# Last value sums behind the first output products, and rows and operands of the next row pairs prepared earlier

## Chip, cores and metric

The kernel runs on one core of one Trainium2 chip. The metric is device time in microseconds (us), from the start to the end of one execution. A core has a matrix engine (TensorE, PE in the profile), a vector engine (VectorE, DVE), an activation engine (ScalarE, ACT), a general engine (GpSimd, POOL) and a queue that starts data transfers (SyncE, SP). Each of them runs its own instructions strictly in the order in which the program issued them, and waits for the others by semaphores.

## What is computed

Two independent blocks over 2048 rows of width 576 are written side by side. Block A is attention with a compressive memory: 32 heads of 18 features, four segments of 512 rows.

```python
for s in range(4):
    logits = qs @ ks.T * scale + mask          # 512 x 512 per head
    a_dot  = softmax(logits) @ vs
    a_mem  = (phi(qs) @ M) / (phi(qs) @ z + 1e-6)
    outs.append(g * a_mem + (1 - g) * a_dot)
    M, z = M + phi(ks).T @ vs, z + phi(ks).sum()
a = concat(outs) @ wo                          # 2048 x 576
```

Block B is the real part of a two-dimensional discrete Fourier transform, written as products with dense matrices:

```python
a, b = x @ hid_re.T, x @ hid_im.T
y = seq_re @ a - seq_im @ b                    # 2048 x 576
out = concat([a_of_block_A, y], axis=-1)
```

## The kernel before

All products of 32-bit numbers are made from two parts each: a high part, rounded to a format that TensorE multiplies at full rate, and a low part, the difference. So the usual three instructions prepare an operand: ScalarE copies the high part, VectorE or GpSimd subtracts it from the original to get the low part.

**Stages.** First come the projections and the memory (`project_qk`, `project_v`, `lookup`). Then one long loop mixes the attention proper with block B: `attention()` is a generator that goes over 64 pairs of heads (a step `p` for each, with eight slots), and after every slot as many pieces of the generator `dense()` (the Fourier products, line 583) are issued as keep the two in step by planned costs. What `dense()` still has left when `attention()` is through is issued by a drain loop, `for t in d: tick()` (line 1215). Last comes `output_stage()`, the product with `wo`.

**The helper `later(n, fn, ...)`** puts an operation off by `n` calls of `tick()`. A `tick()` is called once for every slot and for every piece of the drain loop; `while due: tick()` issues all that is still put off.

**The end of attention.** A group `G` is four heads of one segment. `pv` multiplies probabilities by values into a PSUM tile; `pv_out` (line 1073) makes of it, in five VectorE operations (lines 1083 to 1092), the weighted output of two heads and adds it to the group's tile `og`. After the second pair of a group, `turn_out` (line 1100) transposes `og` in blocks into `ogt` (two VectorE operations), writes it to the DRAM tensor `od[s]`, and copies the last eight columns to `ogl` (GpSimd). After every fourth group `turn_tails` (line 1115) transposes these (`oglt`), writes them to `odt[s]`, and a DMA from DRAM to DRAM brings them, twice, into `od[s]`. So `od[3]` is complete only after the very last of these transfers. The last call of `pv_out` is made in the last step of `attention()`.

**The output stage.** The 16 row tiles are multiplied in pairs: pair `n` is tiles `n` and `n + 8`, so pairs 0 to 3 need the segments 0 and 2 and pairs 4 to 7 need the segments 1 and 3. A pair is multiplied by seven products instead of eight (a Strassen scheme). `o_pair(n)` asks for the rows of a pair, from `od`, into two of the four `craw` buffers, which are used before that for block B's rows; pairs 0 and 1 use other buffers (`oraw`) and are asked for earlier. `left(n)` prepares the pair's left operands in steps (sums of blocks, high and low parts): on VectorE lines 832, 833, 837, 844 and 849, on ScalarE 830, 834, 838, 839, 842 and 845, on GpSimd 829, 836, 841 and 847 (for pair 0 on VectorE). `output_stage` then issues for each `n`, in this order on TensorE, `p1(n)`, `p6(n)`, `p4(n-1)`, `p5(n)`, `p3(n-1)`, `p7(n)`, `p2(n)`: `p1`, `p6` and `p5` are six matmuls each, the others eight. Between them stand the steps of `left(n + 1)` and the operations that take the products out of PSUM: line 877 after `p1` (ScalarE), 883 after `p6`, 889 after `p4`, 900 after `p3`, 907 and 908 after `p7` (VectorE), 914 after `p2` (ScalarE). `p7(n)` writes the same PSUM bank as `p6(n)`, so it has to wait for line 883. Stores go out on SP's queue from line 866.

Of the kernel before, what the change touches and what calls it, by code (L numbers as in the profile page):

```python
# [40 lines left out]
def infini_attention_and_fnet(ctx: ExitStack, tc: tile.TileContext, xT, wqk, w8, wv, wo, beta, xtT, cT, hT, out):  # L41
# [49 lines left out]
    def tick():  # L91
        clock[0] += 1
        for fn, a in due.pop(clock[0], ()):
            fn(*a)
# [595 lines left out]
    def o_pair(n):  # L690
        for t in (n, n + 8):
            o_load(t, lambda: sr.tile([P, 5, P], F32, name="craw", bufs=4))
# [116 lines left out]
    def left(n):  # L809
        one, two = O.pop(n), O.pop(n + 8)  # L810
        add = pool if n else dve
        if n:
            def new():
                return wide.tile([P, 4, P], F32R, name="wide", tag="wide")

            ah, al, s1, s2, l1, l2, a22, tl = (new() for _ in range(8))
            tl = tl[:, :2]
            t = sa.tile([P, 4, 2, P], F32, name="ls", tag="ptt", bufs=2)
        else:
            a, hi, lo = (sa.tile([P, 8, P], F32R, name="l0", tag="pf", bufs=3) for _ in range(3))  # L820
            ah, al, s1, s2, l1, l2 = (x[:, i:i + 4] for x in (a, hi, lo) for i in (0, 4))
            b = sa.tile([P, 6, P], F32R, name="lb", tag="hl", bufs=2)
            a22, tl = b[:, :4], b[:, 4:]
            t = sa.tile([P, 4, 2, P], F32, name="ls", tag="hl", bufs=2)
        LEFT[n] = {"A11": (ah[:, :2], al[:, :2]), "A12": (ah[:, 2:], al[:, 2:]), "A22": (a22[:, :2], a22[:, 2:]),
                   "S1": (s1[:, :2], l1[:, :2]), "S2": (s1[:, 2:], l1[:, 2:]), "S3": (s2[:, :2], l2[:, :2]),
                   "S4": (s2[:, 2:], l2[:, 2:]), 1: tl[:, 0], 2: tl[:, 1]}
        halves = [t[:, i:i + 2].rearrange("p a k x -> p (a k) x") for i in (0, 2)]
        add.tensor_tensor(t[:, 0], two[:, :2], two[:, 2:4], OP.add)
        act.activation(ah, one[:, :4], AF.Copy)  # L830
        yield
        dve.tensor_tensor(t[:, 2], one[:, :2], two[:, :2], OP.subtract)
        dve.tensor_tensor(al, one[:, :4], ah.bitcast(F32), OP.subtract)
        act.activation(a22[:, :2], two[:, 2:4], AF.Copy)
        yield
        add.tensor_tensor(t[:, 1], t[:, 0], one[:, :2], OP.subtract)
        dve.tensor_tensor(a22[:, 2:], two[:, 2:4], a22[:, :2].bitcast(F32), OP.subtract)
        act.activation(tl[:, 0], one[:, 4], AF.Copy)
        act.activation(tl[:, 1], two[:, 4], AF.Copy)
        yield  # L840
        add.tensor_tensor(t[:, 3], one[:, 2:4], t[:, 1], OP.subtract)
        act.activation(s1, halves[0], AF.Copy)
        yield
        dve.tensor_tensor(l1, halves[0], s1.bitcast(F32), OP.subtract)
        act.activation(s2, halves[1], AF.Copy)
        for i, o in enumerate((one, two)):
            add.tensor_tensor(tl[64:, i], o[64:, 4], tl[64:, i].bitcast(F32), OP.subtract)
        yield
        dve.tensor_tensor(l2, halves[1], s2.bitcast(F32), OP.subtract)
        yield  # L850
# [17 lines left out]
    def output_stage():  # L868
        C, Z, U = slice(0, 288), slice(288, 576), {}

        def p1(n):
            u = U[n] = [sb.tile([P, 576], F32, name="u", tag="ab", bufs=10) for _ in range(4)]
            u += [bank("s", [P, L], F32, "s")[:, :288], bank("t", [P, L], F32, "t")[:, :288],
                  ps.tile([P, 288], F32, name="d", bufs=3)]
            seventh(u[4], n, "A11", "B11", True)
            yield
            act.activation(u[0][:, C], u[4], AF.Copy)

        def p6(n):
            u = U[n]  # L880
            seventh(u[5], n, "S2", "T2", True)
            yield
            dve.tensor_tensor(u[0][:, Z], u[5], u[0][:, C], OP.add)

        def p4(n):
            u = U[n]
            seventh(u[5], n, "A22", "T4", tail=(2, 0))
            yield
            dve.tensor_tensor(u[3][:, C], u[5], u[0][:, C], OP.add)
            store(n + 8, u[3], slice(0, D))  # L890

        def p5(n):
            seventh(U[n][6], n, "S1", "T1", True)
            yield

        def p3(n):
            u = U[n]
            seventh(u[6], n, "S4", "B22", tail=(1, 2))
            yield
            dve.tensor_tensor(u[2][:, Z], u[6], u[0][:, Z], OP.add)  # L900
            store(n, u[2], Z if n == 7 else slice(0, D), n == 7)

        def p7(n):
            u = U[n]
            seventh(u[5], n, "S3", "T3", tail=(2, 2))
            yield
            dve.tensor_tensor(u[1][:, C], u[5], u[0][:, C], OP.add)
            dve.tensor_tensor(u[3][:, Z], u[6], u[1][:, C], OP.add)

        def p2(n):  # L910
            u = U[n]
            seventh(u[4], n, "A12", "B21", tail=(1, 1))
            yield
            act.activation(u[2][:, C], u[4], AF.Copy)
            if n == 7:
                store(n, u[2], C)

        for n in range(8):
            todo = [(p1, n), (p6, n), (p4, n - 1), (p5, n), (p3, n - 1), (p7, n), (p2, n)]
            if n == 7:  # L920
                todo += [(p4, n), (p3, n)]
            if n < 6:
                o_pair(n + 2)
            prepare = left(n + 1) if n < 7 else iter(())
            for fn, k in todo:
                if k < 0:
                    continue
                piece = fn(k)
                next(piece)
                next(prepare, None)  # L930
                next(piece, None)
            for _ in prepare:
                pass

# [194 lines left out]
    NP = 2 * NG  # L1129
    SLOTS = (1060.0, 890.0, 1060.0, 660.0, 890.0, 1060.0, 650.0, 1210.0)  # L1130

    def attention():
        for p in range(NP + V_LAG):
            def even(lag, fn, *a):
                if 0 <= p - lag < NP:
                    fn(2 * (p - lag), *a)

            def odd(lag, fn, *a):
                if 0 <= p - lag < NP:
                    fn(2 * (p - lag) + 1, *a)  # L1140

            if p < 2:
                stacks(sq, p + 2)
                OG.append(sa.tile([P, 4, 72], F32, name=f"og{p}"))
            if p == 0:
                value_load(0)
                stack_load(1)
            if p % 2 == 0:
                later(39, value_load, p // 2 + 1)
                later(30, memory_load, p // 2)  # L1150
            even(T_LAG + 1, t_lo, 0)
            odd(F_LAG + 1, f_exp, 2)
            odd(F_LAG + 1, f_split_hi)
            yield SLOTS[0]
            G = p // 2 - 1 if p % 2 == 0 and 0 < p <= NP else None
            even(0, s_fill, 0)
            even(T_LAG, t_fill, 0)
            even(T_LAG, t_fill, 1, G)
            if G is not None and p < T_LAG:
                maxima_transpose(G, bank("trm", [P, L], F32, "t"))  # L1160
            odd(F_LAG + 1, f_split_lo, pool, 512, 1280)
            yield SLOTS[1]
            even(0, s_fill, 1)
            odd(F_LAG + 1, f_split_lo, dve, 0, 512)
            yield SLOTS[2]
            even(V_LAG, pv)
            even(0, s_fill, 2)
            even(T_LAG, t_mask)
            yield SLOTS[3]
            odd(F_LAG, f_fill, 1)  # L1170
            even(T_LAG, t_fill, 2)
            odd(F_LAG, f_fill, 0)
            if p % 2 and p < NP:
                maxima(p // 2)
            yield SLOTS[4]
            odd(F_LAG + 1, f_turn)
            if p % 2:
                stack_load((p + 3) // 2)
                if p < 16:
                    later(2, copy_parts, 2, 8 + p // 2)  # L1180
            elif 4 <= p < 36:
                later(2, copy_parts, 3, (p - 4) // 2)
            even(T_LAG, t_hi)
            yield SLOTS[5]
            odd(V_LAG, pv)
            odd(F_LAG, f_fill, 2)
            odd(F_LAG, f_exp, 1)
            even(T_LAG, t_lo, 1)
            even(T_LAG, t_lo, 2)
            yield SLOTS[6]  # L1190
            odd(F_LAG, f_exp, 0)
            if p >= V_LAG:
                pv_out(p - V_LAG)
            yield SLOTS[7]

# [16 lines left out]
            td += t  # L1212
    while due:
        tick()
    for t in d:
        tick()
    while due:
        tick()
    output_stage()
# [43 lines left out]
```

## Time and profile before

| | us |
|---|---|
| median of three timed runs (995.48 to 996.2) | 995.71 |
| the profiled execution, whole | 997.69 |
| its span, first to last instruction | 996.0 |
| the drain loop's and attention's last products end, about | 931.5 |
| the output stage's products | 931.50 to 991.74 |

The profile is of one execution. Rows of a timeline give the start in us from the span's start, the length, the engine, the line of the kernel, the operation and its output and input tiles, and in brackets the idle time of the engine in front of it with what ended it. Consecutive matmuls overlap in such rows, so a row's length is somewhat more than its share of the engine's time. SPq rows are the issuing of a transfer on the SP queue, not the transfer. In a row of a table by stretches, the columns after the length are the busy time of the engines shown, the granted TensorE clock (1.00 is full speed), the busy share of the DMA engines and GB/s.

### The profile page before, as it was taken

The page shows a single profiled execution, that of the slowest core. Times are in us where ns is not written, and L with a number is a line of the kernel's source. Part 1 is how long each engine was busy: PE and PEld are TensorE (multiplying, and loading weights), DVE is VectorE, ACT ScalarE, POOL GpSimd, SP SyncE. Part 2 cuts the span into 40 slices and gives each one's busy share as a digit, 9 for nine tenths or more (in the row PEclk, how much of TensorE's full clock was granted, in tenths as well). Part 3 has the DMA queues.
Part 4 walks back from the last instruction along what each step waited for, and adds up shares of the span by engine and source line. Part 5 has one row for each costly group of instructions (what it writes and reads, how often), then busy time and mean ns, then how long its engine had stood idle before and what let it go on. Part 6 is the DMA issues. An engine that isn't in the chain of part 4 may idle for free.

```text
span 996.0 us, 25495 instructions
## 1 busy us (share of the span) xinstructions
PE 981.4 (99%) x9246; PEld 918.7 (92%) x9246; DVE 783.2 (79%) x2115; ACT 714.0 (72%) x1687; POOL 672.6 (68%) x744
## 2 busy tenths in 40 slices
PE   9999999999999999999999999999999999999798
PEld 8989989899999999999999999999999999999798
DVE  6657667594678777888898888888889888899775
ACT  6757575653887877878788888877777777877342
POOL 2657676675767677666766777766766767897261
PEclk9999999999999999999999999999999999999999
DMA  7638466767678998899999988789999999988553
GB/s 241 197 120 256 172 181 244 231 232 228 144 182 215 216 247 227 208 235 227 245 234 249 203 223 205 182 197 228 224 227 228 239 232 262 236 189 176 155 183 114
DMA packets 304351, 209.97 MB, mean 211 GB/s; under 512 B 204992, under 2 KB 259136, under 8 KB 304192
## 3 DMA queue, kind: packets, MB, share of 16 engines
q1 hardware_dynamic: 304000, 208.20, 81.1%
q8 instruction: 72, 1.18, 0.5%
q14 instruction: 55, 0.45, 0.2%
q10 hardware_dynamic: 224, 0.14, 0.0%
HBM read 122.37 MB, written 58.98 MB: 182 GB/s over the span
## 4 chain that ended last, share of the span: by engine, by line
PE 82%; DVE 7%; ACT 4%; issue 3%; POOL 2%; DMA 2%; SPq 0%; POOLq 0%; DVEq 0%; ACTq 0%
PE d L583 37%; PE s L952 7%; PE v L84 4%; PE pv L1070 4%; PE qk L250 4%; PE d L630 3%; PE d L628 3%; PE d L629 3%; PE pv L1071 2%; PE t L861 2%; PE m L363 1%; PE t L1026 1%; PE s L861 1%; PE qk L84 1%; PE d L861 1%
## 5 line engine op out<-in xcount | busy, mean ns | idle before, releaser
L958 DVE CUSTOM_DVE_ANT_0 s<-s,causal 128x128 f32<-128x128 f32 (+3 forms) x512 | 248.1, 503 | 94.7 <-PE s L952 85.6
L456 POOL TENSOR_TENSOR clo<-craw,chi 128x512 fp32r<-128x512 f32 x158 | 217.8, 1379 | 90.7 <-ACT chi L451 67.2
L583 PE MATMUL d<-wide,chi 128*128 128x288 f32 x1408 | 262.0, 303 | 0.2
L583 PEld LDWEIGHTS d<-wide,chi 128*128 128x128 f32 x1408 | 210.7, 189 | 2.7 <-issue 0.7
L583 PE MATMUL d<-wide,clo 128*128 128x288 f32 x704 | 173.4, 313 | 0.0
L992 POOL TENSOR_TENSOR hl<-pf,hl 128x768 f16<-128x768 f32 x64 | 114.0, 1781 | 68.2 <-ACT hl L988 55.5
L952 PE MATMUL s<-ks,qs 108*128 108x128 bf16 (+3 forms) x512 | 133.0, 303 | 1.9 <-DVE negm L958 1.6
L1038 ACT ACTIVATE phi<-t 128x384 f16<-128x384 f32 x128 | 61.7, 482 | 101.0 <-PE t L1035 101.0
L981 ACT ACTIVATE pf<-s,nb 128x128 f32<-128x128 f32 (+3 forms) x256 | 128.1, 526 | 6.2
L583 PE MATMUL d<-ab,chi 128*128 128x288 f32 x640 | 123.3, 302 | 0.0
L1053 DVE TENSOR_TENSOR plo<-pf,phi 128x384 f16<-128x384 f32 (+1 forms) x128 | 121.8, 952 | 0.0
L583 PEld LDWEIGHTS d<-wide,clo 128*128 128x128 f32 x704 | 117.9, 189 | 1.4
L1039 ACT ACTIVATE pf<-t 128x384 f32<-128x384 f32 (+1 forms) x192 | 99.6, 519 | 6.6 <-PE t L1026 6.2
L451 ACT ACTIVATE chi<-craw 128x512 fp32r<-128x512 f32 x160 | 100.1, 626 | 3.0 <-DMA craw<-xtT 2.1
L583 PEld LDWEIGHTS d<-ab,chi 128*128 128x128 f32 x640 | 97.9, 189 | 0.5
L988 ACT ACTIVATE hl<-pf 128x768 f16<-128x768 f32 (+1 forms) x128 | 87.4, 730 | 2.0
L583 PE MATMUL d<-ab,clo 128*128 128x288 f32 x320 | 83.1, 308 | 0.0
L628 PE MATMUL d<-wide,chi 128*128 128x288 f32 x256 | 81.4, 318 | 0.0
L630 PE MATMUL d<-wide,clo 128*128 128x288 f32 x256 | 75.7, 296 | 0.9 <-POOL clo L456 0.9
L629 PE MATMUL d<-wide,chi 128*128 128x288 f32 x256 | 75.7, 296 | 0.0
L1053 POOL TENSOR_TENSOR plo<-pf,phi 128x384 f16<-128x384 f32 x64 | 61.7, 965 | 12.1 <-ACT pf L1039 8.7
L992 DVE TENSOR_TENSOR hl<-pf,hl 128x512 f16<-128x512 f32 x64 | 69.3, 1083 | 0.0
(285 smaller groups left out, 2517.2 us busy)
## 6 DMA issues: line engine op xcount, KB each, us to landing
craw<-cT SPq DMA_DIRECT2D x128, 256.0 KB
ks<-kd SPq DMA_DIRECT2D x32, 432.0 KB
qs<-qd SPq DMA_DIRECT2D x32, 432.0 KB
craw<-xtT SPq DMA_DIRECT2D x32, 320.0 KB
vd<-vs SPq DMA_DIRECT2D x16, 440.0 KB
vst<-vd SPq DMA_DIRECT2D x32, 220.0 KB
qd<-p SPq DMA_DIRECT2D x16, 384.0 KB
kd<-p SPq DMA_DIRECT2D x16, 384.0 KB
```

What stands on the lines that cost most here:

```text
L451: act.activation(hi, raw[:, :4], AF.Copy)
L456: engine.tensor_tensor(lo, raw[:, :4], hi.bitcast(F32), OP.subtract)
L583: pe.matmul(o[h], a, b[:, h * 288:h * 288 + 288], start=start, stop=stop)
L628: pe.matmul(o, xh[:, k], wl[k][:, cs], start=k == 0, stop=False)
L629: pe.matmul(o, xh[:, k], wh[k][:, cs], start=False, stop=False)
L630: pe.matmul(o, xl[:, k], wh[k][:, cs], start=False, stop=False)
L952: pe.matmul(o[:, c:c + w], q[:, i * P:w], k[:, :w], start=True, stop=True)
L958: dve.tensor_tensor_reduce(o[:, c:c + w], o[:, c:c + w], CAUSAL[0][:, L - w:], scale=scale, scalar=-LOWEST, op0=OP.add, op1=OP.min, accum_ ...
L981: act.activation(f[:, FIRST_COL[i]:FIRST_COL[i] + w], o[:, c:c + w], AF.Exp, bias=nb[:, i:i + 1], scale=-1.0)
L992: engine.tensor_tensor(hl[:, 1, a:b], f[:, a:b], hl[:, 0, a:b], OP.subtract)
L1039: act.activation(f[:, r:r + w], o[:, :w], AF.Exp, bias=LIFT, scale=SCALE)
L1053: (pool if kind == 2 else dve).tensor_tensor(lo[:, a:b], f[:, a:b], hi[:, a:b], OP.subtract)
```

## The change

The last `pv_out` is no longer called in `attention()`; `output_stage` calls it for `n == 0` behind the matmuls of `p5`, and two `tick()` after each product issue what it puts off (`turn_out`, `turn_tails` and their transfers). The left operands of pair 1 are prepared in the drain loop, step by step, rather than during `n == 0`. The rows of pairs 2 and 3 are asked for in the drain loop, in its first round after all of block B's rows have been split; those of pairs 4 to 7 as before, at the start of `n` = 2 to 5, after everything that was put off has been issued. No operation is added or taken away.

```diff
         for n in range(8):
             ...
-            if n < 6:
+            if 2 <= n < 6:
+                while due:
+                    tick()
                 o_pair(n + 2)
-            prepare = left(n + 1) if n < 7 else iter(())
+            prepare = left(n + 1) if 0 < n < 7 else iter(())
             for fn, k in todo:
                 if k < 0:
                     continue
                 piece = fn(k)
                 next(piece)
                 next(prepare, None)
                 next(piece, None)
+                if n == 0 and fn is p5:
+                    pv_out(NP - 1)
+                tick()
+                tick()
             for _ in prepare:
                 pass
```

```diff
             odd(F_LAG, f_exp, 0)
-            if p >= V_LAG:
+            if V_LAG <= p < NP + V_LAG - 1:
                 pv_out(p - V_LAG)
             yield SLOTS[7]
```

```diff
     while due:
         tick()
+    prepare = left(1)
     for t in d:
         tick()
+        next(prepare, None)
+        if not c_raw and 2 not in O:
+            o_pair(2)
+            o_pair(3)
+    for _ in prepare:
+        pass
     while due:
         tick()
     output_stage()
```

In the changed kernel VectorE's order from the end of pair 0's preparation is: L832 and L833 of pair 1, the dense part's two L653 with L837 between them, L844, L849, the first L883, the five value sums, L907, L908, the two turns into `ogt`, and then pair 2. The turn into `oglt` comes after the L889 of `p4(0)`. On SP the four `craw` loads stand directly behind the `oraw` loads; then follow the store of block B's last rows, `od<-ogt`, a store of `n = 1`, `odt<-oglt`, another store, `od<-odt`, and the two loads of pair 4, of which the second (from segment 3) waits for `od<-odt` to land.

## The prediction

> **What bounds the kernel now.** I read the page first, then the waits of TensorE, then the timelines of TensorE, VectorE, ScalarE, GpSimd and the SP queue from 915 us to the end, because the diff touches only what is issued there: ahead of the drain loop every engine's order is the same in both kernels.
>
> ```profile
> span 996.0 us, 25495 instructions
> PE 981.4 (99%) x9246; PEld 918.7 (92%) x9246; DVE 783.2 (79%) x2115; ACT 714.0 (72%) x1687; POOL 672.6 (68%) x744
> PE t L861 <- DVE u L883: 5.0, 2, 3.1
> ```
>
> TensorE is busy for 99% of the span, so a gain can only be its idle time or its slow time. The last row, from the waits of TensorE over the output stage, says where that idle time is: 5.0 us in two waits, the longer 3.1, both on the VectorE addition at L883. Here are the two on TensorE's own timeline (start, us, instruction, idle before):
>
> ```profile
> 933.09 0.97 PE L861 MATMUL d<-late,l 128*128 128x288 f32 x6
> 935.96 1.07 PE L861 MATMUL t<-late,l 128*128 128x288 f32 x6 [1.90 <-DVE u L883]
> 942.43 0.43 PE L861 MATMUL d<-wide,lb 128*128 128x288 f32 x2
> 946.00 1.80 PE L861 MATMUL t<-late,wide 128*128 128x288 f32 x6 [3.15 <-DVE u L883]
> 954.28 0.95 PE L861 MATMUL t<-late,wide 128*128 128x288 f32 x6
> 960.90 0.95 PE L861 MATMUL t<-late,wide 128*128 128x288 f32 x6
> ```
>
> Call the seventh products of row pair n p7(n). p7(0) starts at 935.96, p7(1) at 946.00, p7(2) at 954.28, p7(3) at 960.90. Between two neighbours lie 50 matmuls (8+8+6+6+8+6+8), and undisturbed they take 960.90 - 954.28 = 6.62 us, 0.132 each. From p7(0) to p7(2) two such rounds would take 13.24 us; they took 18.32. So **5.08 us** are lost there: the idle 3.15, about 0.15 of the pipeline's tail around it, and a slow clock behind it:
>
> ```profile
> 942.85:946.00 3.15, 0.01 (x2) 1.00 0.44 119
> 946.00:949.50 3.50, 3.50 (x15) 0.51 0.39 144
> ```
>
> The third number from the end is the granted clock: 0.51 for 3.5 us after the second wait, 1.00 before it (and after it). The shorter first wait is followed by no such stretch: its six matmuls took 0.12 us more than those of p7(2) (1.07 against 0.95).
>
> What holds L883 back is VectorE's queue, which runs in program order:
>
> ```profile
> 929.98 0.69 DVE L849 TENSOR_TENSOR l<-ls,l 128x512 fp32r<-128x512 f32 x1
> 930.59 0.21 DVE L1083 RECIPROCAL pv<-pv 128x8 f32<-128x8 f32 x1
> 932.25 0.50 DVE L1105 STREAM_TRANSPOSE ogt<-og 128x128 f32<-128x128 f32 x2
> 932.67 0.28 DVE L1117 STREAM_TRANSPOSE oglt<-ogl 128x128 f32<-128x128 f32 x1
> 932.87 0.78 DVE L653 TENSOR_TENSOR y<-y,d 128x288 f32<-128x288 f32 x2
> 933.58 0.82 DVE L832 TENSOR_TENSOR ls<-oraw 128x256 f32<-128x256 f32 x1
> 934.32 1.21 DVE L833 TENSOR_TENSOR wide<-oraw,wide 128x512 fp32r<-128x512 f32 x1
> 935.46 0.45 DVE L883 TENSOR_TENSOR u<-t,u 128x288 f32<-128x288 f32 x1
> 935.82 0.41 DVE L837 TENSOR_TENSOR wide<-oraw,wide 128x256 fp32r<-128x256 f32 x1
> 938.19 0.68 DVE L844 TENSOR_TENSOR wide<-ls,wide 128x512 fp32r<-128x512 f32 x1
> 938.79 0.68 DVE L849 TENSOR_TENSOR wide<-ls,wide 128x512 fp32r<-128x512 f32 x1
> 944.02 0.43 DVE L832 TENSOR_TENSOR ls<-craw 128x256 f32<-128x256 f32 x1 [4.54 <-DMA craw<-od]
> 945.50 0.44 DVE L883 TENSOR_TENSOR u<-t,u 128x288 f32<-128x288 f32 x1
> ```
>
> Ahead of the first L883 stand the last value sums and the turning of their result (930.59 to 932.87), the dense part's last two additions (L653) and two operations that prepare pair 1 (L832, L833). Ahead of the second stands L832 of pair 2, 4.54 us without work until its rows land. Those rows are asked for late, because SP's queue stands still until the turned output exists:
>
> ```profile
> 922.90 1.30 SPq L687 DMA_DIRECT2D oraw<-od  x2
> 932.77 0.33 SPq L94 DMA_DIRECT2D od<-ogt  x1
> 933.20 0.38 SPq L94 DMA_DIRECT2D odt<-oglt  x1
> 934.84 0.70 SPq L94 DMA_DIRECT2D od<-odt  x1
> 936.11 5.31 SPq L687 DMA_DIRECT2D craw<-od  x4
> ```
>
> **The change, part by part.**
>
> *Rows of pairs 2 and 3 asked for in front.* The four craw loads stand directly behind the oraw loads of 922.90. They need the four craw buffers; the last of these is read until the GpSimd row below ends, 926.41.
>
> ```profile
> 925.12 1.29 POOL L456 TENSOR_TENSOR clo<-craw,chi 128x512 fp32r<-128x512 f32 x1 [3.87 <-ACT chi L451]
> 927.00:928.00 1.00, 1.00 (x20) 1.00 0.37 108
> 928.00:929.00 1.00, 1.00 (x10) 1.00 0.02 5
> 942.85 0.63 ACT L830 ACTIVATE wide<-craw 128x512 fp32r<-128x512 f32 x1 [4.05 <-DMA craw<-od]
> ```
>
> So they go out between 924.2 and about 926.5, some ten microseconds sooner. The DMA engines are nearly empty from 928 (5 GB/s), so nothing is pushed aside; the oraw rows are in front of them and are in by about 928. The slowest landing on record, 936.11 to 942.85 = 6.74 us behind the turned output, would put pair 2 in at 933.2; it is wanted when VectorE reaches its L832, near 938. Cost nothing; the second wait goes. Saved: 5.08 us, clock stretch included. If the cover failed by x us, x would come back.
>
> *Pair 1 made in the drain loop, value sums behind p5(0).* On VectorE the work in front of the first L883 loses the span 930.59 to 932.87 (five sums, two ogt turns, one oglt turn: 2.28 us) and gains L837, L844 and L849 of pair 1: 0.41 + 0.60 (938.19 to 938.79) + 0.68 = 1.69. Net 0.59 us sooner, so p7(0) at 935.37. GpSimd's three operations for pair 1 can start at 928 instead of 932.56; their length is 934.99 - 932.56 = 2.43 us:
>
> ```profile
> 932.56 0.74 POOL L829 TENSOR_TENSOR ls<-oraw 128x256 f32<-128x256 f32 x1
> 934.20 0.79 POOL L841 TENSOR_TENSOR ls<-oraw,ls 128x256 f32<-128x256 f32 x1
> L832 DVE TENSOR_TENSOR ls<-oraw x2: 411/617/823, 926.6 to 933.6; 128x256 f32<-128x256 f32 x2
> ```
>
> The same L832 took 0.41 us without GpSimd running and 0.82 beside it, L833 0.68 by L849's rows of the same size and 1.21 beside it: about 0.9 us of drag in all. Wherever those three operations fall, some VectorE work beside them is dragged, so I leave the 0.9 where it is. Bounds: drag gone, 1.5 us sooner; drag doubled, 0.3 later (nothing gained).
>
> *What stands behind the moved work.* L883 ends near 935.3, the five sums (930.59 to 932.25, 1.66) near 937.0, then L907 and L908 and the turns, 938.3. TensorE wants L907's bank at p4(0), 28 matmuls after 935.37: 939.1, against 937.5. L832, L833 and L883 of pair 1's round follow (0.82 + 1.21 + 0.45), done 940.8; p7(1) wants them at 935.37 + 6.62 = 942.0, slack 1.2 us. On GpSimd the ogl copy now stands in front of pair 2's L829 and waits for the sums: pair 2's three operations end near 939.7, and p6(2) needs what follows from them near 944.9. Hidden, both.
>
> *The added wait on SP.* The od<-ogt, odt and od<-odt writes now stand behind the four loads, between the stores of n=1, and the load of row tile 12 (segment 3) waits for od<-odt to land; behind it on SP stand two stores and the loads of pair 5. oglt now follows L837 and L889 (0.41 and about 0.45 behind the 940.8 above), so odt goes out near 942.1, od<-odt 1.64 us later (933.20 to 934.84), 943.7. Its own landing shows nowhere; by the nearest rows it takes between 1.64 and 6.74. A load takes
>
> ```profile
> 955.46 1.03 SPq L687 DMA_DIRECT2D craw<-od  x2
> 960.18 0.73 POOL L829 TENSOR_TENSOR ls<-craw 128x256 f32<-128x256 f32 x1 [0.60 <-DMA craw<-od]
> ```
>
> 960.18 - 955.46 = 4.72 us, or 6.74 at worst. So tile 12 lands between 950.1 and 957.2; I take 3.1 for od<-odt, nearer the small write than a pair of loads, and 951.5. p7(3) then comes at 935.37 + 3 x 6.62 = 955.2 and needs L832, L833, L883 (1.6 to 2.5 us) after that landing: due 952.7 to 953.6. Hidden by one to two microseconds, the thinnest cover of the change.
>
> The Trainium skill speaks against this step: DMA: Bandwidth & Descriptors, section Rules for kernel authors, says a DMA whose outermost dimension is under 16 is confined to that many engines, and od<-odt has an outermost 4. By its sixteenth of 436 GB/s for each engine and its 2.0 us fixed part, 256 KB would take an estimated 4.4 us, landing tile 12 at 952.8, still about in time. No row here shows that transfer alone.
>
> **Sum.** 5.08 + 0.59 = 5.67 us. The profiled execution took 997.69 us (span 996.0); the median of the timed runs is 1.98 lower, 995.71, which I take as base: **990.0 us**; the changed kernel's span would be 990.3.
>
> **Rivals.**
> - *The slow clock is not in the timed runs.* The profiled execution is 1.98 us over the median, and the slow stretch costs 5.08 - 3.15 - 0.15 = 1.8. If the timed runs never had it, the gain is 3.9 and the time 991.8. For it: the likeness of the two sizes. Against: a profile costs something anyway, and 3.15 us of idle time stands in every run. The Trainium skill, TensorE: Matmul & The Clock Gate, section What's actually happening, tells of a free-running window of about 3.4 us, so that it may differ from run to run; the trace, with 0.51 after 3.15 us and 1.00 after 1.90, does not contradict it.
> - *The first wait stays.* The drag doubles, or pair 1's chain through GpSimd and ScalarE ends L849 later: gain 5.1, 990.6; if p7(1) also loses a microsecond to the sums in front of it, 991.6.
> - *Tile 12 comes late: slower.* In-order SP stands at its load, VectorE at L832 of pair 4, TensorE at p7(3). A landing at 957.2, the upper bound, means a wait of up to 957.2 + 2.5 - 955.2 = 4.5 us, longer than 3.15, so the slow clock too: 6.3 lost, 996.3. It decides from a wait of 3.9. A landing at 955 costs 1.4 to 2.3: 991.4 to 992.3.
> - *It doesn't do what it says.* If the four loads stood still on SP until where they go out now, only 0.59 is left: 995.1. Nothing in SP's order shows a reason; what blocked them stands behind them now.
>
> **How the numbers follow.** Forecast 0.62 (own range 989.1 to 991.2); clock not in the timed runs 0.14; first wait stays 0.10; tile 12 somewhat late 0.07; late enough to cost as much as is gained 0.04; no effect 0.03. The range: low is 995.71 - 5.08 - 1.5 = 989.1, less 0.3 for the spread of runs, 988.8; high is 992.3, the partial case of tile 12, which takes in the clock case. Faster by over 0.2% (2.0 us, what a measurement of this kernel can tell from no change) is all but the last two and a little of the fourth: 0.92; within 0.2%: 0.04; slower: 0.04.
>
> **What would show it.** TensorE's wait on L883 once, 1 to 1.5 us, p7(0) near 935.4, and none before p7(1); granted clock 1.00 in every stretch to 985; craw<-od x4 on SP starting near 924; the five sums right after the first L883; TensorE's last matmul near 986 instead of 991.7. Wrong: a wait before p7(3) behind "DMA craw<-od", a stretch at half clock, or p7(1) held by L883 with the five sums in front of it.

## The result, and the profile after

| us | before | changed |
|---|---|---|
| median of 22 timed runs each, taken together | 996.34 | **994.11** |
| lowest and highest of these | 995.48 to 999.83 | 992.41 to 996.36 |
| the profiled execution, whole | 997.69 | 994.13 |
| its span | 996.0 | 992.4 |

The ratio is 0.997, 95% interval 0.996 to 0.9979. The change makes the kernel faster, but by 2.2 us of the median rather than by 5.7, and 994.11 lies above the forecast range (988.8 to 992.3).

The page of the changed kernel and TensorE's waits over the output stage:

```profile
span 992.4 us, 25495 instructions
PE 980.9 (99%) x9246; PEld 918.3 (93%) x9246; DVE 786.4 (79%) x2115; ACT 714.7 (72%) x1687; POOL 675.2 (68%) x744
PE t L861 <- DVE u L883: 1.9, 1, 1.9
```

One of the two waits on L883 is gone, the longer one. The other has the length it had. TensorE's timeline shows where (start, us, instruction, idle before):

```profile
932.91 0.96 PE L861 MATMUL s<-wide,l 128*128 128x288 f32 x6
937.38 1.06 PE L861 MATMUL t<-late,l 128*128 128x288 f32 x6 [1.91 <-DVE u L883]
944.11 0.95 PE L861 MATMUL t<-late,wide 128*128 128x288 f32 x6
950.75 0.95 PE L861 MATMUL t<-late,wide 128*128 128x288 f32 x6
957.36 0.95 PE L861 MATMUL t<-late,wide 128*128 128x288 f32 x6
986.98 1.23 PE L861 MATMUL d<-wide 128*128 128x288 f32 x8
```

The five rows from 937.38 on are p7(0) to p7(3) and the last matmuls. From p7(0) to p7(2) they take 13.37 us, against 18.32 in the profile of before and 13.24 undisturbed: of the 5.08 us, 4.95 are gone in this execution, and p7(1) and p7(3) wait for nothing. But the stage starts with the first row, p1(0), at 932.91; in the profile of before this was 931.50. From p1(0) to p7(0) lie 4.47 us, against 4.46.

The SP queue, and what it leads to on VectorE at row tile 12 (L832 of pair 4, then the L883 that p7(3) needs):

```profile
924.18 1.24 SPq L687 DMA_DIRECT2D oraw<-od  x2
925.52 4.27 SPq L687 DMA_DIRECT2D craw<-od  x4
943.80 0.38 SPq L94 DMA_DIRECT2D odt<-oglt  x1
945.69 0.70 SPq L94 DMA_DIRECT2D od<-odt  x1
954.56 0.43 DVE L832 TENSOR_TENSOR ls<-craw 128x256 f32<-128x256 f32 x1 [1.61 <-DMA craw<-od]
956.06 0.44 DVE L883 TENSOR_TENSOR u<-t,u 128x288 f32<-128x288 f32 x1
```

The four loads go out ten microseconds earlier than in before (936.11), as planned. Tile 12 is the one load that VectorE still waits for, 1.61 us; L883 ends at 956.50 and p7(3) starts at 957.36, so 0.86 us of cover is left.

### The profile page after: what moved, and what is told of

Its sections match the earlier page's. It is cut to its first block, busy times and chain, and to the rows that moved or that the text cites. A ratio compares the mean times of both kernels' runs of the same rounds, so it can differ in the third digit from the quotient of the medians.

```text
span 992.4 us, 25495 instructions
## 1 busy us (share of the span) xinstructions
PE 980.9 (99%) x9246; PEld 918.3 (93%) x9246; DVE 786.4 (79%) x2115; ACT 714.7 (72%) x1687; POOL 675.2 (68%) x744
## 4 chain that ended last, share of the span: by engine, by line
PE 84%; DVE 7%; ACT 4%; DMA 2%; issue 2%; POOL 1%; SPq 0%; POOLq 0%; DVEq 0%; ACTq 0%
PE d L583 38%; PE s L958 7%; PE v L84 4%; PE pv L1076 4%; PE qk L250 4%; PE d L628 3%; PE d L629 3%; PE d L630 3%; PE t L861 2%; PE pv L1077 2%; PE m L363 1%; PE d L861 1%; PE s L861 1%; PE t L1032 1%; PE qk L84 1%
```

## Experiments

Each time is the median of its runs; the ratio is to runs of before on the same chip. Two theories stood at the start. The *clock theory*: the slow clock follows either of the two waits, in some executions only; before hides it when it follows the first wait, the changed kernel cannot. The *drag theory*: the first wait stays because operations on VectorE and GpSimd that now lie beside each other slow each other down. They do not exclude each other. The letters A and B in the expectations stand for another pair of theories each time.

**Both kernels once more** (no edit).

> The kernel before, unchanged, for the spread of its spans and granted clocks. Theory A (the half-clock stretch behind the 3.15 us wait is in every execution): mean granted clock 0.997 to 0.998 in all, spans within 1 us of 996.0 apart from a few long ones. Theory B (it is in some executions only, and the base of the prediction, 995.71, was the kind without it): two kinds of execution, spans near 994 with clock 0.999 to 1.000 and spans 1.5 to 2 us longer with 0.997 to 0.998, the waits of TensorE on line 883 (1.9 and 3.15 us) alike in both.

997.68 us (995.63 to 999.39, 12 runs), ratio 0.9999 (0.9986 to 1.0012). Neither theory of the expectation is what came: there are two kinds of execution, but the shorter ones do not have the full clock (0.997 to 0.999). The profiled execution took 995.86, and is another case than the one that the prediction read. TensorE's timeline, and a table by stretches (us, busy time of PE, PEld, DVE, ACT and POOL left as they are, then granted clock, DMA share, GB/s):

```profile
935.97 1.08 PE L861 MATMUL t<-late,l 128*128 128x288 f32 x6 [1.90 <-DVE u L883]
945.72 1.06 PE L861 MATMUL t<-late,wide 128*128 128x288 f32 x6 [1.30 <-DVE u L883]
952.46 0.95 PE L861 MATMUL t<-late,wide 128*128 128x288 f32 x6
937.00:940.45 3.45, 3.45 (x17) 3.45 (x16) 2.12 (x4) 0.41 (x1) 0.00 (x0) 0.51 0.62 195
```

Here the clock is at half for about 3.4 us **one microsecond behind the first wait**, and full behind the second. TensorE thereby reaches p7(1) later, but that one waits for the rows of pair 2 anyway: its wait is 1.30 instead of 3.15, and p7(0) to p7(2) takes 16.49 rather than 18.32.

> The changed kernel, unchanged, for another profile and for its spread (its 22 timed runs went from 992.41 to 996.36, their clocks from 0.996 to 1.000). Theory A (the spread is TensorE's clock, which falls in some executions behind a wait of about 1.9 us): an execution of 992.4 to 993 with clock 1.000 has no slow stretch, one of 994 or more has a stretch near 0.5 with no new wait. Theory B (the spread is the landing of row tile 12): in the longer executions TensorE waits 1 us or more in front of p7(3), VectorE behind DMA craw<-od.

993.56 us (992.66 to 994.99, 7 runs), ratio 0.9963 (0.9949 to 0.9977). The profile has p1(0) at 931.45, the first wait at 1.89 us and 13.37 us from p7(0) to p7(2), at full clock. Four runs with a mean clock of 0.999 or more took 992.7 to 993.6; the three with 0.998 took 994.5 to 995.0.

**Single executions of both**, without an edit, to see which kinds there are.

> The kernel before once more, for a profile. Theory A (one drop, either hidden in the second wait or behind it, and the landing of the turned output decide the time): near 995.7 with the half-clock stretch behind the first wait and a second wait under 2 us; near 997.7 with the stretch behind the second wait, which is then 3 us or more; over 998.5 with odt landing more than 3 us after its issue. Theory B: times that do not go with these.

> The kernel before a fourth time, for another profile; the same conditions as for the look before it.

> The changed kernel once more, for a profile. Theory A: if the time is over 994, a stretch of about 3.4 us at half clock begins within 1.5 us behind the first wait, and the way from p7(0) to p7(2) takes 14.9 us instead of 13.2; if under 993.6, no such stretch. Theory B: a time over 994 without it, with a wait in front of p7(3) or a later p1(0).

> The changed kernel once more, for a profile of one of its longer executions (994 to 996.4 us), of which none was caught so far. Theory A (the 1.9 us wait before p7(0) is followed in these by a stretch at half clock that nothing absorbs): if this execution takes 994 us or more with a mean clock of 0.998 or less, the granted clock falls to 0.5 to 0.75 for about 3.4 us some 1 us behind p7(0), and p7(0) to p7(2) takes about 15.0 us (13.23 + 1.66 to 1.8) instead of 13.37. Rival C (the longer executions lose their time before the output stage): clock 1.00 throughout the stage, 13.37, and p1(0) at 934 or later. If it takes under 993.9 with a clock of 0.999 or more: 13.37, and nothing is told apart.

> As after_look3: 15.0 us from p7(0) to p7(2) with a stretch at half clock behind the wait (Theory A), or 13.37 and a stage that starts at 934 or later (Rival C), where the execution takes 994 us or more.

> As after_look3: 15.0 us from p7(0) to p7(2) with a stretch at half clock behind the wait (Theory A), or 13.37 and a stage that starts at 934 or later (Rival C), where the execution takes 994 us or more.

They took 999.7 and 995.75 (before), 993.86, 994.27, 994.46 and 992.92 (changed). before_look2 did not go with its expectation: over 998.5, but od<-odt went out 1.63 us behind odt as in the others, and the clock was at half for two stretches in a row. The ten profiled executions, worked out from TensorE's timelines and the granted clock:

| | time | p1(0) starts | first wait | second wait | p7(0) to p7(2) | half clock |
|---|---|---|---|---|---|---|
| before | 997.69 | 931.50 | 1.90 | 3.15 | 18.32 | behind the second |
| before_again | 995.86 | 931.52 | 1.90 | 1.30 | 16.49 | behind the first |
| before_look2 | 999.70 | 932.52 | 1.88 | 2.90 | 19.32 | behind the second, twice as long |
| before_look3 | 995.75 | 930.91 | 1.89 | 3.33 | 16.97 | none |
| after | 994.13 | 932.91 | 1.91 | none | 13.37 | none |
| after_again | 992.66 | 931.45 | 1.89 | none | 13.37 | none |
| after_look2 | 993.86 | 932.68 | 1.88 | none | 13.37 | none |
| after_look3 | 994.27 | 931.23 | 2.19 | none | 14.91 | behind the first |
| after_look4 | 994.46 | 931.68 | 1.91 | none | 14.90 | behind the first |
| after_look5 | 992.92 | 931.63 | 1.95 | none | 13.37 | none |

The execution of before without half clock, before_look3, is the one that the sums below start from (p1(0), p7(0), p7(1), p7(2)):

```profile
930.91 0.96 PE L861 MATMUL s<-wide,l 128*128 128x288 f32 x6
935.36 1.07 PE L861 MATMUL t<-late,l 128*128 128x288 f32 x6 [1.89 <-DVE u L883]
945.59 1.07 PE L861 MATMUL t<-late,wide 128*128 128x288 f32 x6 [3.33 <-DVE u L883]
952.33 0.95 PE L861 MATMUL t<-late,wide 128*128 128x288 f32 x6
```

Two executions of the changed kernel can be laid side by side: in both p7(0) starts at 936.14, after the same wait. The first two rows are from after_look4, with p7(0) and p7(2) on TensorE's timeline and the stretch between them:

```profile
936.14 1.79 PE L861 MATMUL t<-late,l 128*128 128x288 f32 x6 [1.91 <-DVE u L883]
951.04 0.95 PE L861 MATMUL t<-late,wide 128*128 128x288 f32 x6
936.14:939.60 3.46, 3.46 (x14) 3.46 (x15) 2.59 (x9) 0.00 (x0) 1.62 (x3) 0.51 0.03 7
```

The same three of after_look5:

```profile
936.14 1.06 PE L861 MATMUL t<-late,l 128*128 128x288 f32 x6 [1.95 <-DVE u L883]
949.51 0.95 PE L861 MATMUL t<-late,wide 128*128 128x288 f32 x6
936.14:939.60 3.46, 3.46 (x26) 3.46 (x27) 3.29 (x10) 1.04 (x3) 1.64 (x3) 1.00 0.02 7
```

In the same 3.46 us TensorE began 14 instructions at a clock of 0.51, and 26 at 1.00. That costs 1.53 us by p7(2), and the two times differ by 1.54. So half clock behind the first wait costs the changed kernel 1.5 us, and rival C, a loss ahead of the stage, falls for this difference. It stays for others: 994.13 and 993.86 were reached without half clock, with p1(0) at 932.91 and 932.68. No execution over 994.5 was profiled, so why some timed runs took 994.9 to 996.4 is not shown.

**What decides whether half clock follows.** This can be read from the same traces. In every profile the clock also falls behind the last matmul, and a fall in the stage lies a whole number of 3.413 us ahead of that one (after_look4: 936.20 and 990.81, 16 x 3.413 = 54.61). So the changes lie on the borders of steps of 3.413 us, which can be laid over every execution. Single steps (us, busy time of PE, granted clock, DMA share, GB/s), the first two from after_look4, then one from after and two from before_look3:

```profile
932.78:936.20 3.42, 1.51 (x12) 1.00 0.22 86
936.20:939.61 3.41, 3.41 (x14) 0.50 0.03 5
935.58:938.99 3.41, 1.61 (x12) 1.00 0.24 91
940.54:943.95 3.41, 1.72 (x13) 1.00 0.76 211
943.95:947.37 3.42, 1.78 (x13) 1.00 0.09 26
```

The first step holds 1.91 us without matmuls, and half clock follows. The step from after holds 1.80, and none follows. The second wait of before_look3, 3.33 us long, lies across a border, 1.69 and 1.64, and none follows. In all 17 profiles a step at full clock with 1.90 us or more without matmuls is followed by half clock, and one with 1.80 or less is not. Half clock lasts for two steps where the first of them still holds 0.60 us or more without matmuls (before_look2, and pair1_early_sums_old below with 1.11), and for one where it holds 0.19 or less. So what a wait of 1.9 us costs depends on where it lies in a step. This is read from the traces; no run moved a wait within the steps on purpose. The Trainium skill, TensorE: Matmul & The Clock Gate, section What's actually happening, describes a free-running activity window of 3413 ns, so that the point of a change depends on how the window lies. The traces agree, with steps of 3.413 us that lie differently in each execution.

**Rows asked for sooner, alone.** In before:

```diff
-            if n < 6:
+            if 2 <= n < 6:
                 o_pair(n + 2)
 ...
     for t in d:
         tick()
+        if not c_raw and 2 not in O:
+            o_pair(2)
+            o_pair(3)
```

> Only the rows of pairs 2 and 3 are asked for in the drain loop; value sums and pair 1 stand where they stood before. Theory A (the second wait is worth all of the gain, the other two parts nothing together): the second wait of TensorE on line 883 (3.15 us) is gone, the first (1.9) stays, time within 0.7 us of the changed kernel's. Theory B (the other two parts bring something): 0.6 us or more above the changed kernel.

994.41 us (993.7 to 996.36, 12 runs), ratio 0.9972 (0.9962 to 0.9983). The edit did less than its expectation assumed: the turned output was issued ahead of the drain loop, so the loads still stand behind od<-odt and pass only one store. They start at 935.18 instead of 936.11. That microsecond is enough to show the clock theory in another kernel (TensorE's timeline and the stretch):

```profile
935.50 1.22 PE L861 MATMUL t<-late,l 128*128 128x288 f32 x6 [1.90 <-DVE u L883]
943.90 1.07 PE L861 MATMUL t<-late,wide 128*128 128x288 f32 x6
936.40:939.75 3.35, 3.35 (x16) 3.35 (x15) 2.11 (x4) 0.41 (x1) 0.00 (x0) 0.51 0.75 221
```

The half clock behind the first wait delays TensorE just until the rows are in, and the second wait is gone. The five of the twelve runs with a mean clock of 1.0 took 994.4 to 995.3, no less than most of the others, as it has to be if the stretch costs nothing here. The median lies 0.85 us above after_again, which ran beside it; the intervals overlap, so the two theories of the expectation are not told apart by it.

**The first wait filled** with 12 matmuls whose result is not used, in the changed kernel and in before:

```diff
         def p5(n):
+            if n == 0:
+                hi, w = LEFT[0]["A11"][0], WO["B11", 0][0]
+                for _ in range(12):
+                    pe.matmul(U[0][6], hi[:, 0], w, start=True, stop=True, skip_group_check=True)
             seventh(U[n][6], n, "S1", "T1", True)
```

> The changed kernel with 12 matmuls more, without effect, between p6(0) and p5(0): 1.59 us of work put into the first wait of TensorE (1.9 us). Theory A (the spread of the changed kernel comes from the clock, which falls to half behind this wait in some executions): the wait shrinks to about 0.3 us, the clock never falls, all executions have clock 0.999 to 1.000 and lie between 992.3 and 993.7; median 0.3 to 1.2 us below the changed kernel's. Theory B (the spread comes from elsewhere, transfers or the stages ahead): spread and median as in the changed kernel, 992.4 to 996, or 1.6 us later.

993.36 us (992.54 to 993.96, 6 runs), ratio 0.996 (0.9945 to 0.9975). The wait that is left is 0.60 us. The clock is 0.999 or 1.0 in all six runs, and none is above 994: the changed kernel's runs from 994 to 996.4 are not there. The wait was forecast at 0.3 and the highest run at 993.7.

> The kernel before with the same 12 matmuls. Theory A (in the kernel before, a clock that falls behind the first wait costs nothing, because the second wait ends when the rows of pair 2 have landed, not earlier; the half-clock stretch only eats into that wait): with the first drop gone, the second wait is the full 3.1 us and the drop falls behind it, in most executions 997 to 998.5, hardly any near 995.7, so slower than before though TensorE's first wait is filled. Theory B (each drop costs 1.7 us wherever it is): median 0.5 to 1.5 us below the kernel before.

1000.28 us (999.04 to 1001.93, 11 runs), ratio 1.0034 (1.0023 to 1.0044). Filling a wait makes this kernel slower, as the clock theory says, though by more than it said: mean clock 0.996 to 0.997 in all runs. In the profile the second wait is longer, and the clock falls behind it:

```profile
935.69 1.07 PE L861 MATMUL t<-late,l 128*128 128x288 f32 x6 [0.21 <-DVE u L883]
947.19 1.81 PE L861 MATMUL t<-late,wide 128*128 128x288 f32 x6 [4.61 <-DVE u L883]
932.92 0.38 SPq L94 DMA_DIRECT2D odt<-oglt  x1
936.30 0.70 SPq L94 DMA_DIRECT2D od<-odt  x1
```

The last two rows, of the SP queue, hold what no theory expected: od<-odt follows odt after 3.38 us; in the profile of before it was 1.64 (933.20 to 934.84). With it the rows come later: from p1(0) to p7(1) it takes 15.85 us, against 14.68 in before_look3, which has no half clock, and from p7(1) to p7(2) 8.18 against 6.74. So of this profile's loss 1.17 us are the late rows and 1.44 the clock. Why the small write took longer here was not tried.

**Pair 1 made late again**, the rest of the change kept:

```diff
-            prepare = left(n + 1) if 0 < n < 7 else iter(())
+            prepare = left(n + 1) if n < 7 else iter(())
 ...
-    prepare = left(1)
     for t in d:
         tick()
-        next(prepare, None)
 ...
-    for _ in prepare:
-        pass
```

> The changed kernel with pair 1 prepared during n = 0 again (its five VectorE operations no longer all ahead of the first L883), rows and value sums as changed. Theory A (what was won by moving the value sums was given back by the pair-1 operations put ahead of L883, and by VectorE and GpSimd slowing each other there): L883 waits only for y, L832 and L833, the first wait of TensorE falls from 1.9 to 0 to 0.6 us, perhaps 1 us comes back at p6(1), which needs L844; 0.3 to 1.5 us below the changed kernel. Theory B (the first wait is set by something else, pair 0 or ScalarE): wait still 1.5 us or more, time within 0.4 us of the changed kernel.

**991.95 us** (991.23 to 992.97, 6 runs), ratio 0.9944 (0.9928 to 0.996), the best of the kernels that compute all. On TensorE the first wait is gone, and a short one on pair 1's L844 stands in its place:

```profile
934.10 1.04 PE L861 MATMUL t<-late,l 128*128 128x288 f32 x6
937.80 0.80 PE L861 MATMUL t<-late,wide 128*128 128x288 f32 x4 [0.28 <-DVE wide L844]
```

The clock is 0.999 or 1.0 in all six runs. So the early pair 1 is what keeps the 1.9 us wait in the changed kernel, and it costs 1.6 us of the median against after_again, which ran beside it. With p7(0) sooner, tile 12 comes just too late: p7(3) waits 0.17 us for its L883.

**Pair 1 made sooner, alone**: the change without its lines on `pv_out` and without the two `tick()` after each product.

> Rows early and pair 1 in the drain loop, but the last value sums where they were, ahead of L883. Theory A (pair 1's three further VectorE operations cost about 1.7 us in front of L883 plus up to 0.7 of drag): first wait of TensorE 3.6 to 4.3 us, half clock behind it, 2 to 4 us above the version with rows alone, that is 996.4 to 998.4. Theory B (they fill time in which VectorE would wait anyway): first wait 1.9 to 2.5, within 0.7 us of rows alone.

996.68 us (995.31 to 998.59, 10 runs), ratio 0.9995 (0.9984 to 1.0006): no difference from before, and 2.3 us above rows_alone, as Theory A of the expectation says. The loads go out at 935.11, as in rows_alone; the first wait is 3.77 us, the clock falls to half in its last 1.1 us and stays there for 6.8 us, and the second wait is gone. What the rows win, the longer first wait takes.

**The value sums moved, alone**: the change's lines on `pv_out` and the `tick()` calls in before; pair 1 and the requests as before.

> The kernel before with nothing changed but the place of the last value sums (behind p5(0), with what follows from them); rows of pairs 2 and 3 asked for when the output stage reaches n = 0 and 1, pair 1 prepared during n = 0, as before. On SP the four loads stand behind block B's last store, no longer behind od<-ogt, odt and od<-odt. Theory A (moving the sums is what frees SP's queue; asking in the drain loop adds nothing): loads go out near 933, pair 2 lands by 938, no wait of TensorE over 0.5 us, clock 1.000, time within 0.5 us of the version with sums and rows (991.95). Theory B (the early request is worth something of its own): VectorE waits for DMA craw<-od in front of pair 2's L832, second wait of TensorE 1 us or more, 993 to 994.5.

992.4 us (991.4 to 993.15, 6 runs), ratio 0.9952 (0.9935 to 0.9968). Since nothing that was put off now stands in front of the four loads, they go out at 933.68, early enough; p7(0) comes at 934.94 without a wait. Asking for the rows in the drain loop as well gives 991.95, lower by 0.45 us, but the intervals overlap widely, so a gain from it is not shown. Theory A missed one thing: TensorE waits 0.61 us in front of p7(3), because tile 12 lands too late for the earlier p7(0).

**Pair 1's block sums taken from GpSimd**: in the changed kernel, for pair 1, the three operations L829, L836 and L841 become ScalarE copies. This kernel leaves out the block sums and differences of pair 1, so it serves for the times alone.

```diff
+        def combine(o, x, y, op):
+            if n == 1:
+                act.activation(o, x, AF.Copy)
+            else:
+                add.tensor_tensor(o, x, y, op)
-        add.tensor_tensor(t[:, 0], two[:, :2], two[:, 2:4], OP.add)
+        combine(t[:, 0], two[:, :2], two[:, 2:4], OP.add)
```

> The changed kernel with GpSimd's three sums and differences for pair 1 (L829, L836, L841) replaced by copies of their first operand on ScalarE, so these parts of pair 1 are left out. Theory A (VectorE's subtractions of two SBUF operands take longer while GpSimd runs its own, and this drag, 1.66 us in the changed kernel against 0.93 before, ate the 0.59 us): VectorE's L847, L849, L832 and L833 fall back to 0.49 (two), 0.69, 0.41 and 0.68, first wait of TensorE 0.2 to 0.7 us. Theory B (the first wait is held by the chain through ScalarE, L845 and L877): drag or no drag, the first wait stays over 1.4 us.

991.38 us (990.99 to 991.95, 4 runs), ratio 0.9942 (0.9925 to 0.9959). The same VectorE operations in the two kernels, first in the changed one, with GpSimd's beside them:

```profile
930.87 0.92 DVE L847 TENSOR_TENSOR lb<-oraw,lb 64x128 fp32r<-64x128 f32 x2
931.82 1.12 DVE L849 TENSOR_TENSOR l<-ls,l 128x512 fp32r<-128x512 f32 x1
932.86 0.96 DVE L832 TENSOR_TENSOR ls<-oraw 128x256 f32<-128x256 f32 x1
933.74 0.95 DVE L833 TENSOR_TENSOR wide<-oraw,wide 128x512 fp32r<-128x512 f32 x1
936.88 0.45 DVE L883 TENSOR_TENSOR u<-t,u 128x288 f32<-128x288 f32 x1
930.16 1.27 POOL L829 TENSOR_TENSOR ls<-oraw 128x256 f32<-128x256 f32 x1 [2.34 <-DMA oraw<-od]
931.51 0.88 POOL L836 TENSOR_TENSOR ls<-ls,oraw 128x256 f32<-128x256 f32 x1
932.47 1.07 POOL L841 TENSOR_TENSOR ls<-oraw,ls 128x256 f32<-128x256 f32 x1
```

and then in pair1_copies, where the lines are six further down (L853 is L847, L889 is L883):

```profile
930.02 0.49 DVE L853 TENSOR_TENSOR lb<-oraw,lb 64x128 fp32r<-64x128 f32 x2
930.54 0.69 DVE L855 TENSOR_TENSOR l<-ls,l 128x512 fp32r<-128x512 f32 x1
931.15 0.42 DVE L838 TENSOR_TENSOR ls<-oraw 128x256 f32<-128x256 f32 x1
931.49 0.69 DVE L839 TENSOR_TENSOR wide<-oraw,wide 128x512 fp32r<-128x512 f32 x1
934.36 0.45 DVE L889 TENSOR_TENSOR u<-t,u 128x288 f32<-128x288 f32 x1
934.86 1.05 PE L867 MATMUL t<-late,l 128*128 128x288 f32 x6 [0.41 <-DVE u L889]
```

Four operations of 3.95 us take 2.29 without GpSimd's sums beside them: a drag of 1.66 us, most of the first wait, which falls from 1.91 to 0.41. The drag theory, which is Theory A of this expectation, is shown. The Trainium skill, GPSIMD Engine Reference, section Key points, says that GpSimd shares its SBUF interfaces with VectorE, with contention where a VectorE instruction has two SBUF inputs. All four have that, and the size is this run's.

## Why the prediction was wrong

**The sum: a loss from one kind of execution, a base from another.** This is the step that cost most. The 5.08 us were read from an execution of 997.69 us, in which half clock followed the second wait, and were taken off 995.71, the median of three runs. The prediction laid the 1.98 us between the two to the profiling, and took 3.15 us of idle time to stand in every run. But the second wait is 1.30 to 3.33 us in the profiles of before, and an execution of 995.75 or 995.86 is profiled too, and has no such stretch behind its second wait: it loses 16.97 - 13.24 = 3.73 or 16.49 - 13.24 = 3.25 there. The two ways of doing it right agree. Taken off its own execution, the profile's loss gives 997.69 - 18.32 + 13.37 = 992.74, 2.70 above the 990.04 of the sum: 1.98 for the base, 0.59 for the first wait, 0.13 between 13.24 and 13.37. A loss of 16.97 - 13.37 = 3.60 from before_look3 gives 992.15; the difference, again 0.59, is the later p1(0) of the first (931.50 against 930.91). Executions of the changed kernel without a slow stretch took 992.4 to 994.1. The rival *the slow clock is not in the timed runs* had this right in its size (991.8), at a chance of 0.14; what it calls "the timed runs" was the lower half of them only. Of the 22 runs of before beside the changed kernel 11 lie from 995.48 to 996.23, and 11 from 996.44 to 999.83.

**"Followed by no such stretch": a stretch at half clock behind the first wait was taken to be out of the question.** That was read from one execution, in which the 1.90 us of the first wait lie across the border of two steps, 1.74 and 0.16. It occurs in two of six profiles of the changed kernel (1.53 us by p7(2)) and in one of four of before, where the second wait swallows it. The change took away the wait that hid it. In the 22 timed runs of the changed kernel, the eight with a mean clock of 0.999 or more that took less than 993.5 and one at 994.13 stand beside 13 with 0.998 or less, from 993.79 to 996.36. So the median is 994.11; the nine alone have 992.74.

**The first wait was to be 0.59 us shorter and is not.** 2.28 us of sums and turns left VectorE's queue in front of L883, and L837, L844 and L849 came in with about 1.55 (1.69 in the prediction). The drag was left where it was, 0.94; it is 1.66. Together -2.28 + 1.55 + 0.72 = -0.01, and the wait went from 1.90 to 1.91. In before GpSimd's three sums ran beside transposes and L653, and only L832 and L833 suffered. Started at 930.16, they run beside four operations that read two SBUF tiles each. This was the rival *the first wait stays*, and the lower bound given for this term ("drag doubled, nothing gained") is what came.

**Tile 12** landed about one microsecond later than taken: from od<-odt's start to L832 8.87 us (945.69 to 954.56), against 3.1 + 4.72 = 7.82. On the prediction's clock, in which p7(0) is 2.01 us sooner (935.37 against 937.38), that is 952.55 instead of 951.5. The 952.8 estimated from the Trainium skill (DMA: Bandwidth & Descriptors, section Rules for kernel authors) was nearer, though no row shows od<-odt alone, and the 2.0 us in that estimate are the page's for transfers that GpSimd issues, not SP. The cover held in all six profiles of the changed kernel, with 0.38 (after_look2) to 1.54 us (after_look3) left, and the rival on the slower side did not come. It is the next limit: without the first wait the cover is gone (0.17 us of waiting in pair1_late, 0.61 in sums_behind_only). The prediction's "slowest landing", 6.74 us, was not the slowest either: VectorE's L832 had its rows only at 944.02, 7.91 us after the request. Nothing hung on it here.

**What was right:** the loads at 925.5, the second wait gone with all of its 3.15 us, the five sums behind the first L883 hidden (937.24 to 938.98 in the changed profile), p7(1) held by nothing: 944.11 - 937.38 = 6.73, against 6.62.

**Does it add up?** From before_look3, without a slow stretch, the times of the changed kernel's profiles follow by three terms: less 3.60, plus the later start of p1(0), plus what the clock costs. after_look5: 995.75 - 3.60 + 0.72 = 992.87 (992.92 measured). after_look4: 995.75 - 3.60 + 0.77 + 1.53 = 994.45 (994.46). The profile after: 995.75 - 3.60 + 2.00 = 994.15 (994.13). after_again and after_look2 come out as closely; after_look3 needs its longer first wait (2.19, so 0.30 more) as a fourth term: 995.75 - 3.60 + 0.32 + 0.30 + 1.54 = 994.31 (994.27). **Open** is why p1(0) starts anywhere from 930.91 to 932.91; both kernels show it (930.91 to 932.52 before, 931.23 to 932.91 after), and no run was made for it. The traces show where it arises: the same matmuls, counted from the first, start 0.89 us later in after than in before_look3 at 10 us, 1.77 at 244 us and 1.99 at 909 us. That is ahead of the drain loop, where both kernels issue the same, so it is no effect of the change.

## What to carry to other kernels

Before a stall or a slow stretch of one profile is taken off a median, look at a second and a third execution: the loss and the base have to be of the same kind, or the loss has to be taken off its own execution's time. A wait for a transfer hides losses ahead of it up to its own length, so whoever removes it pays for these from then on; look for them (here an idle time of 1.9 us with half clock behind it) and remove them together. Work that is moved forward costs more than its duration if it stands in front of the critical instruction on an in-order engine or beside work of another engine that slows it: here the half of the change that moved sums back gained (992.4 alone), and the half that moved pair 1 forward gave part of it up again (991.95 without it).

## What the runs showed of the hardware

- The clock changed only at the borders of steps of 3.413 us. It fell to half behind each step with 1.90 us or more without matmuls and behind none with 1.80 or less, for 3.4 us or, behind waits of 2.90 and 3.77 us, for 6.8. The fall came a microsecond into the next work (before_again), nearly at once (after_look4) or while TensorE still waited (pair1_early_sums_old); 3.33 us without matmuls, across a border, passed without any (before_look3). The Trainium skill, TensorE: Matmul & The Clock Gate, section Why this matters for your kernels, asks for no idle gap over some 3 us; here gaps of 1.9 us were followed by a drop in after_look3's, after_look4's, before_again's and rows_alone's executions (2.19 us in the first), and so were not safe.
- VectorE and GpSimd slow each other: a subtraction of two SBUF tiles took 0.96 instead of 0.42 us (128x256) and 0.95 to 1.12 instead of 0.69 (128x512, 1.21 in before), and GpSimd's sums 0.88 to 1.27 in the changed kernel against 0.74 to 0.79 in before.
- A 12-matmul filler that only kept TensorE busy made one kernel steadier (992.54 to 993.96) and the other slower (1000.28), by the wait that each has behind it.
